# Three token blocks instead of two share each group of first-layer weights, fewer weight tiles are prepared during attention, and attention's output copy moves ahead of the logarithm

## The chip, the cores and the metric

The kernel runs on one core of a Trainium2 chip. The metric is the device time of one execution in microseconds (us). The engines are called PE (matmul), PEld (PE's weight loads), DVE (vector), ACT (scalar activation), POOL (GpSimd) and SP (which here only issues DMAs).

## What is computed

A gated linear attention is followed by two feed-forward layers. The first uses a rational function of the hidden values, the second h times its cosine. The reference, cut to the core:

```python
for t in range(S):                                   # S = 768, B = 4, H = 8, D = 48
    state = alpha[:, :, t, :, None] * state + np.einsum('bhd,bhe->bhde', k[:, :, t], v[:, :, t])
    y[:, :, t] = np.einsum('bhd,bhde->bhe', q[:, :, t], state)
x = y.transpose(0, 2, 1, 3).reshape(B * S, H * D)    # 3072 x 384
h = x @ w_in                                         # 384 -> 2048, weights are float64
P = a[0] + a[1] * h + a[2] * h * h + a[3] * h * h * h
Q = 1.0 + np.abs(b[0]) * np.abs(h) + np.abs(b[1]) * h * h
x = (P / (Q + 1e-06)) @ w_out                        # 2048 -> 384
h = x @ w_in2
out = (h * np.cos(h)) @ w_out2
```

## The kernel before

**Attention** is cut into 24 units (6 chunks of 128 time steps by 4 batches), one unit per slot; slots are numbered n = -3 to 24. A slot's PE work is `scores` (L332), `y_state` (L399), `y_scores` (L409), `update0` (L366) and `transposes` (L354). POOL scales q (L323) and k (L318) and masks two score tiles (L346). DVE and ACT do the decay, its inverse and the copies, and `y_out` (L425) copies a unit's output out of PSUM.

**The first layer** works on 6 blocks of 512 tokens and 16 features (tiles of 128 hidden columns), so it has 96 layer steps n = 0 to 95. Step 0 runs in slot 20: slots 20 to 24 hold attention and layer steps 0 to 4 (LEAD = 20). A step's PE work is `gemm1(n)` (L562: 9 matmuls, three passes for each of 3 parts of the contraction, with x and w split into a high and a low part) and, five steps later, `gemm2` of that tile (L578: 9 matmuls into the three accumulators `acc`). Between the two stands `rational`: on ACT an absolute value, a scaled copy, a logarithm and an exponential (L636, L637, L645, L646) and a rounding (L608); on DVE L628, L631, L632, L633 and L640; on POOL L638, L639 and L613. `gemm1` writes one of four PSUM banks in turn. The bank of tile n - 3 is free once L633 has run in step n, and `gemm1(n + 1)` waits for that.

**The order of blocks.** Blocks 0 and 1 take turns: 11 features of block 0, the same 11 of block 1, then 5 and 5 (`H1 = 11`), so that a feature's weights serve two blocks. A block that is left before its last feature has its sums copied from PSUM to SBUF by ACT (L593), and at its end DVE adds them to the new sums (L597). Blocks 2 to 5 run all 16 features in a row.

**Weights** come as 64-bit floats, a tile at a time (384 KB, one feature of `w_in` or `w_out`). Each is fetched by `w_fetch` (L174) and converted in three "ticks" by `to_f32`: two ACT operations (L72, L73), then DVE L77, then DVE L78. `w_hi` (L215, ACT) rounds it and `w_lo` (L225, POOL) takes the rest. L73 writes a bank that L77 and L78 read. The list `SOME` says how many tiles are fetched in each slot up to 20; from step 5 to step 31 each layer step runs two ticks, so a tile takes a step and a half. Raw tiles land in `spare` (four places) or in `raw` (two).

**The next block's input** is loaded by `x_load`, and split by `x_hi` (L702, ACT) and `x_lo` (L706, DVE), one third in each of three steps: for block 1 in steps 5 to 7, for block 2 in steps 28 to 30.

The order on every engine is the order of the program text; nothing is reordered. DVE, ACT and POOL each run their instructions strictly in a row.

Of the kernel before, what the change touches and what calls it, by code (L numbers as in the profile page):

```python
# [24 lines left out]
NU = NC * B  # L25
H1 = 11
NO = 0
SOME = [0, 0] + 5 * [1, 1, 0] + [1, 1, 1, 2]

# [13 lines left out]
def attn_then_two_moe(ctx, tc, kqT, aT, vP, w1i, w1o, ma, mb, w2i, w2o, out):  # L43
# [70 lines left out]
    kq_t = [kq_all[:, i] for i in range(5)]  # L114
    v_t = [const.tile([128, H * D + 64 - D], F32, tag=f"v{i}", name=f"v{i}") for i in range(4)]
    st_all = const.tile([128, 4, DM], F32, tag="st", name="st")
# [7 lines left out]
    def w_tile(s, f):  # L124
        ws[s][f] = wp.tile([128, 2, DM], F32R, tag=f"w{s}_{f}", name=f"w{s}_{f}")

    w_order = sorted(
        [(0, s, i) for i in range(NF) for s in range(2)],
        key=lambda w: (w[2] + 5 * w[1] + (H1 if w[2] >= H1 else 0), w[1])
    ) + [(1, s, i) for s in range(2) for i in range(NF)]  # L130
    ready = set()
    late = {}
    for i, (_, s, f) in enumerate(w_order[:2 * NF]):
        u = KEEP + i - (2 * NF - (NU - KEEP))
        if u >= KEEP:
# [16 lines left out]

    def in_spare(i):
        return i < sum(SOME[:-1]) and i % 6 < 4

    def w_fetch(upto):

        i = fetched[0]
        fetched[1] = upto
        more = LEAD + 5 <= slot[0] < LEAD + N1  # L160
        most = 4 if more else 2
        if i >= upto or len(steps) > 5 or sum(not in_spare(j) for j in range(i - len(steps), i + 1)) > most:
            return
        w = w_order[i]
        fetched[0] += 1
        if in_spare(i):
            flat = spare[:, 2 * DM * (i % 6):2 * DM * (i % 6 + 1)]
        elif more and i % 4 < 2:
            if not raw_a:
                raw_a.append(const.tile([128, 3 * HP * (C + 1)], I32, tag="a", name="raw_a"))  # L170
            flat = raw_a[0][:, 2 * DM * (i % 2):2 * DM * (i % 2 + 1)]
        else:
            flat = raw_p.tile([128, 2 * DM], I32, tag="raw", name="raw")
# [12 lines left out]
    def tick(k, ahead=0):  # L186

        while k and steps and (len(steps) > ahead or fetched[0] == fetched[1]):
# [8 lines left out]
            if i == 2:  # L197
                steps.pop(0)
                stage[w] = t
                to_hi.append(w)  # L200

    def early(m, s, i):

        return NF * s + i if m == 1 and NF * s + i < NF + NO else None

    def w_hi():
        while to_hi:
            m, s, i = w = to_hi.pop(0)
            at = early(m, s, i)
            if ws[s][i] is None:  # L210
                w_tile(s, i)
            hi = ws[s][i][:, 0]
            if at is not None:
                hi = kq_t[at % 3][:, 1].rearrange("p a b -> p (a b)")[:, :DM].bitcast(F32R)
            nc.scalar.activation(out=hi, in_=stage[w], func=AF.Copy)  # L215
            to_lo.append((w, hi))

    def w_lo(engs):
        engs = list(engs)
        while to_lo:  # L220
# [222 lines left out]
    def convert(n, place):  # L443

        if place == 0:
            turn[:] = [0] * 5 if n < 2 else [1, 1, 1, 0, 0]
            if n >= LEAD + 2:
                turn[:] = [1, 1, 1, 0, 1] if n == LEAD + 2 else [1, 0, 1, 0, 1 if n < NU else 0]
            if n == MORE:
                turn[4] = 1  # L450
            if n == MORE + 1:
                turn[:] = [2, 0, 0, 3, 0]
        assert n != LEAD + 2 or place or not steps[0][1]
        tick(turn[place], 2 if n < LEAD else 1)
        turn[place] = 0
# [68 lines left out]
    def where(n):  # L524
        m, r = divmod(n, N1)
        if n < 2 * H1:
            return 0, *divmod(n, H1)
        if n < 2 * NF:
            blk, f = divmod(n - 2 * H1, NF - H1)
            return 0, blk, H1 + f  # L530
        return m, *divmod(r, NF)

    def in_parts(m, blk):
        return m == 0 and blk < 2

# [17 lines left out]
    def gemm1(n):  # L553
        m, blk, f = where(n)
        assert m or (0, 0, f) in ready
        h = h_bank(n)
        x = xt[m, blk]
        i = 0
        for kk in range(NK):
            ks = slice(kk * 128, (kk + 1) * 128)  # L560
            for w, xx in PASSES:
                nc.tensor.matmul(h, ws[0][f][:, w, ks], x[:, xx, kk, :], start=i == 0, stop=i == 8)  # L562
                i += 1
        T[n] = {"h": h}

    def gemm2(n):
        m, blk, f = where(n)
        d = T.pop(n)
        assert m or (0, 1, f) in ready
        first = f == 0 or in_parts(m, blk) and f == H1  # L570
        last = f == NF - 1 or in_parts(m, blk) and f == H1 - 1
        for k in range(NK):
# [10 lines left out]

    outs = []

    def acc_out(most=NK):

        while outs and most:
# [25 lines left out]

    def rational(n):

# [17 lines left out]
        if one:  # L634
# [39 lines left out]
    def x_load(m, blk, kk):  # L674
        if kk == 0 and (m, blk) not in xt:
            xt[m, blk] = x_p.tile([128, 2, NK, TB], F32R, tag="x", name="x")
        x = xt[m, blk][:, 1, kk, :].bitcast(F32)
        ks = slice(kk * 128, (kk + 1) * 128)
# [21 lines left out]
    def x_hi(m, blk, kk):  # L700
        x = xt[m, blk]
        nc.scalar.activation(out=x[:, 0, kk, :], in_=x[:, 1, kk, :].bitcast(F32), func=AF.Copy)  # L702

    def x_lo(m, blk, kk, eng=None):
        hi, lo = (xt[m, blk][:, i, kk, :] for i in range(2))
        (eng or nc.vector).tensor_tensor(out=lo, in0=lo.bitcast(F32), in1=hi.bitcast(F32), op=ALU.subtract)  # L706
# [151 lines left out]
    def w_first(t, a, e, r):  # L858
# [16 lines left out]
        elif t == 3:  # L875
            v = [const.tile([128, 3 * 128], F32R, tag=f"v{i}", name=f"w_v{i}") for i in range(4)]
            hi, lo = v[:2], v[2:]
# [349 lines left out]

    def layers(n):
        slot[0] = n + LEAD
# [14 lines left out]
        rational(n)  # L1244
        cosine_parts(n)
# [14 lines left out]
        i = n - (N1 - NF)  # L1260
        if n < 2 * NF:
# [25 lines left out]
    with tc.manual_schedule():  # L1287
# [17 lines left out]
        for n in range(-3, NU + 1):  # L1305
# [221 lines left out]
```

## Time and profile before

| | before |
|---|---|
| median of 3 runs | 913.98 us (913.88 to 915.51) |
| the profiled execution, its own time | 913.8 us |
| its span, first to last instruction | 912.1 us |
| PE busy, share of the span | 892.4 us, 98% |
| PE's weight loads | 741.2 us, 81% |
| DVE, ACT, POOL busy | 693.9, 697.1, 702.9 us (76%, 76%, 77%) |
| chain that ended last | PE 72%, DVE 8%, ACT 7%, POOL 6%, DMA 4% |

Busy PE time counts overlapping matmuls once, so 98% says only that a matmul was nearly always under way. How well PE is fed is read from the starts of equal pieces of work: of `scores` in attention, of `gemm1` in the layers.

### The profile page before, as it was taken

What the parts mean: (1) busy time and instruction counts of PE and PEld (TensorE: products, weight loads), DVE (VectorE), ACT (ScalarE), POOL (GpSimd) and SP (SyncE); (2) the same over time, 40 slices, a digit from 0 to 9 for tenths busy, and PEclk for the clock granted to TensorE, in tenths of its full rate; (3) what the DMA queues carried; (4) which work ended last, traced back from release to release, by engine and by line L of the source; (5) the groups of instructions that cost most, each with busy time, mean ns of one, the idle gap of its engine ahead of it and who ended that gap; (6) DMA issues with size and microseconds to landing.
All of it is one profiled execution on the core that took longest, in us unless ns stands there. A gap on an engine that the chain in (4) does not pass through costs nothing.

```text
span 912.1 us, 16494 instructions
## 1 busy us (share of the span) xinstructions
PE 892.4 (98%) x5732; PEld 741.2 (81%) x5732; DVE 693.9 (76%) x1247; ACT 697.1 (76%) x1302; POOL 702.9 (77%) x699
## 2 busy tenths in 40 slices
PE   7999999999999999999999999999999999999997
PEld 7788777887788888888888888878888888888885
DVE  7989799998999989989979767666366554555552
ACT  5999898989889788888788778656577666666653
POOL 6899998999889888889879668669787475655332
PEclk9999999999999999999999999999999999999999
DMA  8999545211233141232165276630243433533432
GB/s 281 357 366 370 191 124 196 82 63 36 104 107 94 57 142 45 87 107 94 53 205 185 95 238 239 202 110 27 74 134 109 161 113 96 167 102 105 139 105 90
DMA packets 67307, 128.87 MB, mean 141 GB/s; under 512 B 6928, under 2 KB 30224, under 8 KB 67216
## 3 DMA queue, kind: packets, MB, share of 16 engines
q1 hardware_dynamic: 67216, 127.74, 43.1%
q8 instruction: 47, 0.77, 0.4%
q14 instruction: 44, 0.36, 0.1%
HBM read 95.21 MB, written 32.51 MB: 140 GB/s over the span
## 4 chain that ended last, share of the span: by engine, by line
PE 72%; DVE 8%; ACT 7%; POOL 6%; DMA 4%; issue 2%; SPq 0%; DVEq 0%; ACTq 0%
PE acc L578 22%; PE b L562 18%; PE acc L1054 15%; PE b L1019 6%; PE r L1019 5%; PE r L562 4%; POOL kq L323 2%; POOL kq L318 2%; DMA kq<-kqT 2%; DVE g L628 1%; DVE z L631 1%; ACT b L645 1%; DVE g L640 1%; DMA a<-aT 1%; PE b L1198 1%
## 5 line engine op out<-in xcount | busy, mean ns | idle before, releaser
L578 PE MATMUL acc<-hi,w 128*128 128x512 f32 x738 | 252.5, 396 | 0.0
L562 PE MATMUL b<-x,w 128*128 128x512 f32 x927 | 233.8, 397 | 1.3 <-DVE g L633 1.1
L613 POOL TENSOR_TENSOR lo<-g,hi 128x512 fp32r<-128x512 f32 x128 | 170.2, 1330 | 66.2 <-ACT hi L608 59.4
L562 PEld LDWEIGHTS b<-x,w 128*128 128x128 f32 x927 | 173.4, 188 | 45.4 <-DVE g L633 4.1
L578 PEld LDWEIGHTS acc<-hi,w 128*128 128x128 f32 x738 | 138.7, 188 | 33.9
L1111 POOL TENSOR_TENSOR lo<-g,hi 128x512 fp32r<-128x512 f32 x64 | 83.0, 1297 | 103.6 <-ACT hi L1110 91.6
L578 PE MATMUL acc<-lo,w 128*128 128x512 f32 x369 | 145.7, 395 | 0.0
L639 POOL TENSOR_TENSOR z<-z,ah 128x512 f32<-128x512 f32 x96 | 124.7, 1299 | 8.0
L1054 PE MATMUL acc<-hi,w_out 128*128 128x512 f32 x384 | 130.3, 395 | 0.0
L608 ACT ACTIVATE hi<-g 128x512 fp32r<-128x512 f32 x128 | 80.4, 628 | 47.8 <-PE acc L578 32.6
L578 PEld LDWEIGHTS acc<-lo,w 128*128 128x128 f32 x369 | 69.4, 188 | 16.5
L638 POOL TENSOR_SCALAR z<-ah,cq 128x512 f32<-128x512 f32 x96 | 74.4, 775 | 5.5 <-ACT ah L636 5.4
L1054 PE MATMUL acc<-lo,w_out 128*128 128x512 f32 x192 | 76.4, 398 | 0.4 <-POOL lo L1111 0.2
L1054 PEld LDWEIGHTS acc<-hi,w_out 128*128 128x128 f32 x384 | 68.7, 188 | 9.9
L640 DVE TENSOR_TENSOR g<-g,b 128x512 f32<-128x512 f32 x72 | 49.1, 682 | 16.2 <-ACT g L637 16.0
L636 ACT ACTIVATE ah<-b 128x512 f32<-128x512 f32 x72 | 42.8, 594 | 19.9 <-PE b L562 19.6
L562 PE MATMUL r<-x,w 128*128 128x512 f32 x225 | 56.8, 397 | 1.0 <-DVE g L633 1.0
L1096 DVE SCALAR_TENSOR_TENSOR ah<-z,b 128x512 f32<-128x512 int32 x44 | 30.2, 685 | 35.9 <-ACT z L1092 35.9
L637 ACT ACTIVATE g<-b,cq 128x512 f32<-128x512 f32 x72 | 56.1, 779 | 0.0
L633 DVE SCALAR_TENSOR_TENSOR g<-g,cq,b 128x512 f32<-128x512 f32 x72 | 53.9, 748 | 2.5
L628 DVE SCALAR_TENSOR_TENSOR g<-g,cq,b 128x512 f32<-128x512 f32 x72 | 53.4, 742 | 0.5
L645 ACT ACTIVATE b<-z,lnb 128x512 f32<-128x512 f32 x72 | 50.1, 696 | 4.7 <-DVE g L628 4.0
(202 smaller groups left out, 2028.7 us busy)
## 6 DMA issues: line engine op xcount, KB each, us to landing
w_out<-wd SPq DMA_DIRECT2D x64, 384.0 KB, 3.1
kq<-kqT SPq DMA_DIRECT2D x24, 512.0 KB, 6.6
w<-wd SPq DMA_DIRECT2D x16, 384.0 KB, 3.1
wd<-w SPq DMA_DIRECT2D x16, 384.0 KB, 2.6
a<-aT SPq DMA_DIRECT2D x23, 258.0 KB, 5.8
raw<-w2o SPq DMA_DIRECT2D x14, 384.0 KB, 3.9
v<-vP SPq DMA_DIRECT2D x24, 192.0 KB, 6.6
x<-x1d SPq DMA_DIRECT2D x18, 256.0 KB, 4.2
```

The source lines that it names most:

```text
L562: nc.tensor.matmul(h, ws[0][f][:, w, ks], x[:, xx, kk, :], start=i == 0, stop=i == 8)
L578: nc.tensor.matmul(acc[k], ws[1][f][:, w, ks], d[g], start=first and i == 0, stop=last and i == 2)
L608: nc.scalar.activation(out=t["hi"], in_=t["g"], func=AF.Copy)
L613: eng.tensor_tensor(out=t["lo"], in0=t["g"], in1=t["hi"].bitcast(F32), op=ALU.subtract)
L628: nc.vector.scalar_tensor_tensor(g, g, cq[:, 3:4], two["h"], ALU.add, ALU.mult)
L638: nc.gpsimd.tensor_scalar(zz, ah, cq[:, 1:2], cq[:, 0:1], ALU.mult, ALU.add)
L639: nc.gpsimd.tensor_tensor(out=zz, in0=zz, in1=ah, op=ALU.mult)
L640: nc.vector.tensor_tensor(out=g, in0=g, in1=h, op=ALU.mult)
L645: nc.scalar.activation(out=r, in_=two["z"], func=AF.Ln, scale=LN_S, bias=lnb)
L1019: nc.tensor.matmul(tile[:, half], w[p], x[q], start=start and i == 0, stop=True, skip_group_check=True)
L1054: nc.tensor.matmul(acc[k], item["w"][:, w, ks], item[g], start=first, stop=last)
L1111: nc.gpsimd.tensor_tensor(out=p["lo"], in0=p["g"], in1=p["hi"].bitcast(F32), op=ALU.subtract)
```

## The change

The three first blocks take turns, over 6, 5 and 5 features (`TURN = 3`, `OFFS`), so blocks 0 to 2 fill steps 0 to 47. Sums that leave PSUM after the first group are copied by ACT (9 copies, in steps 11, 17 and 23), after the second group DVE adds them to what is stored (9 adds, steps 28, 33 and 38), after the third DVE adds and writes the result (9 adds, steps 43, 48 and 53). Before there were 6 copies (steps 16 and 27) and 6 adds (steps 32 and 37), and block 2's result was copied by ACT.

Fetches of slots 2, 3, 5 and 19 and one of two in slot 20 go; raw tiles land in the weight tile's own place. First-layer conversion runs on to step 37, the second layer's starts in step 44 (`S2`). A step that splits x, or that follows an add, runs one tick instead of two. Block 1's x is split in steps 3 to 5 and is wanted by `gemm1(6)`; block 2's in steps 9 to 11 and is wanted by `gemm1(12)`; block 2's x lies in the places of attention's `a` and `v`.

`y_out` of slots 20 to 24 is issued inside `rational`, between the scaled copy and the logarithm.

```diff
-H1 = 11
+H1 = 6
+OFFS = 0, 6, 11, NF
-SOME = [0, 0] + 5 * [1, 1, 0] + [1, 1, 1, 2]
+TURN = 3
+S2 = 44
+SOME = [0] * 6 + 5 * [1, 0, 1]
...
+            flat = wp.tile([128, 2 * DM], I32, tag=f"w{w[1]}_{w[2]}", name="raw")
...
             if f < NF - 1:
-                nc.scalar.activation(out=part(blk, k), in_=acc[k], func=AF.Copy)
+                if group(f) == 0:
+                    nc.scalar.activation(out=part(blk, k), in_=acc[k], func=AF.Copy)
+                else:
+                    added[0] = slot[0]
+                    nc.vector.tensor_tensor(out=part(blk, k), in0=part(blk, k), in1=acc[k], op=ALU.add)
                 continue
...
+        if between:
+            between()
         if two:
             r = two["h"]
             nc.scalar.activation(out=r, in_=two["z"], func=AF.Ln, scale=LN_S, bias=lnb)
...
-        if n < NF:
-            nxt, at, load = (0, 1), n - 5, n == 3
-        elif n < 2 * NF:
-            at, load = n - 2 * NF + 4, n == 2 * NF - 6
+        if n < 2 * NF:
+            nxt, at, load = ((0, 1), n - H1 + 3, n == 0) if n < H1 else ((0, 2), n - 9, n == H1)
...
-        if n < 2 * NF:
+        if n < S2:
             if n > 1:
-                tick(2 if n > 4 else 1, 1)
+                tick(2 if n > 4 and not split and added[0] < slot[0] else 1, 1)
         elif n < N1 - NF:
             if not split:
-                tick(1, 1)
+                tick(2 if added[0] < slot[0] else 1, 1)
...
-                layers(n - LEAD)
-                y_out(n - 1)
+                layers(n - LEAD, partial(y_out, n - 1))
```

On POOL in attention, slots 7 and 8 (`kq<-kq,p` is the scaling of q, `kq<-kq,z` of k, `w<-st` the low part of a weight tile), before:

```order
L323 TENSOR_TENSOR kq<-kq,p 128x512
L318 TENSOR_TENSOR kq<-kq,z 128x512
L225 TENSOR_TENSOR w_0_110<-st,w_0_110 128x384
L346 AFFINE_SELECT hi<-hi 128x512
L346 AFFINE_SELECT lo<-lo 128x512
L323 TENSOR_TENSOR kq<-kq,p 128x512
L318 TENSOR_TENSOR kq<-kq,z 128x512
L225 TENSOR_TENSOR w_1_111<-st,w_1_111 128x384
L346 AFFINE_SELECT hi<-hi 128x512
L346 AFFINE_SELECT lo<-lo 128x512
```

The weight operation is gone from slots 7, 8 and 10 and from one place in slot 21; the first one now stands in slot 11, and from there to slot 20 the pattern is that of before.

On ACT in slot 22, layer step 2 (`ah<-b` is the absolute value, `b<-z,lnb` the logarithm, `yo<-y` the output copy of `y_out`, `hi<-sc` the next slot's first mask copy), now:

```order
L657 ACTIVATE ah<-b_1905 128x512
L658 ACTIVATE g<-b_1905,cq 128x512
L435 ACTIVATE yo<-y 128x512
L668 ACTIVATE b_1830<-z,lnb 128x512
L669 ACTIVATE b_1830<-b_1830 128x512
L225 ACTIVATE w_3_2006<-st 128x384
L75 ACTIVATE st<-raw 128x384
L76 ACTIVATE r_2011<-raw 128x384
```

Before, the copy stood behind the last of these, five instructions later.

On DVE in steps 27 and 28 (`g<-g,cq,b` first is L628 of before, the fourth of a step is L633, `st<-raw` the last tick of a weight tile, `kq<-kq,acc` the new adds), now:

```order
L649 SCALAR_TENSOR_TENSOR g<-g,cq,b_3065 128x512
L652 SCALAR_TENSOR_TENSOR z<-z,b_3024 128x512
L653 SCALAR_TENSOR_TENSOR b_3024<-z,b_3024 128x512
L654 SCALAR_TENSOR_TENSOR g<-g,cq,b_3024 128x512
L661 TENSOR_TENSOR g<-g,b_3109 128x512
L81 SCALAR_TENSOR_TENSOR st<-raw,r_3150 128x384
L613 TENSOR_TENSOR kq<-kq,acc_3005 128x512
L613 TENSOR_TENSOR kq<-kq,acc_3009 128x512
L613 TENSOR_TENSOR kq<-kq,acc_3013 128x512
L649 SCALAR_TENSOR_TENSOR g<-g,cq,b_3109 128x512
L652 SCALAR_TENSOR_TENSOR z<-z,b_3065 128x512
```

The three adds stand ahead of step 28's first operation, so everything of that step on DVE, the operation that frees PE's bank among it, comes after them.

## Rows read from the trace of the kernel before

**Rows 1.** Windows: PE, PEld, DVE, ACT, POOL busy, clock, DMA share, GB/s.

```profile
60.00:80.00 20.00, 18.96 (x391) 16.86 (x389) 17.79 (x49) 18.48 (x38) 19.72 (x23) 1.00 1.06 332
160.00:180.00 20.00, 20.00 (x87) 16.14 (x86) 19.29 (x32) 18.75 (x36) 18.75 (x19) 1.00 0.30 86
```

**Rows 2.** Timeline of PE in attention, `scores` alone: start, length, [idle before <-releaser].

```profile
61.10 1.10 PE L332 MATMUL sc<-kq 48*64 48x128 f32 x32 [0.35 <-POOL kq L318]
65.07 1.10 PE L332 MATMUL sc<-kq 48*64 48x128 f32 x32
69.67 1.10 PE L332 MATMUL sc<-kq 48*64 48x128 f32 x32 [0.34 <-POOL kq L318]
```

**Rows 3.** Timeline of POOL in attention, slots 4 to 12, single operations.

```profile
29.82 1.28 POOL L323 TENSOR_TENSOR kq<-kq,p 128x512 f32<-128x512 f32 x1 [0.58 <-DMA kq<-kqT]
...
35.56 1.27 POOL L323 TENSOR_TENSOR kq<-kq,p 128x512 f32<-128x512 f32 x1 [2.05 <-DMA kq<-kqT]
...
64.97 1.00 POOL L225 TENSOR_TENSOR w<-st,w 128x384 fp32r<-128x384 f32 x1
```

**Rows 4.** DMA queues, 20 to 100 us: packets, MB, share of 16 engines.

```profile
q1 hardware_dynamic: 14997, 28.13, 99.7%
```

**Rows 5.** Timeline of PE and ACT, slots 22 and 23.

```profile
114.27 1.09 PE L399 MATMUL y<-kq,s 48*64 48x128 f32 x16 [1.34 <-ACT yo L425]
...
113.63 0.59 ACT L425 ACTIVATE yo<-y 128x512 f32<-128x512 f32 x1
```

**Rows 6.** Timeline of DVE, layer steps 4 and 5.

```profile
119.92 0.74 DVE L628 SCALAR_TENSOR_TENSOR g<-g,cq,b 128x512 f32<-128x512 f32 x1
...
122.02 0.75 DVE L633 SCALAR_TENSOR_TENSOR g<-g,cq,b 128x512 f32<-128x512 f32 x1
...
127.44 1.14 DVE L706 TENSOR_TENSOR x<-x 128x512 fp32r<-128x512 f32 x1 [0.58 <-ACT x L702]
```

**Rows 7.** Timeline of PE, `gemm1` of steps 6, 11, 27, 28, 29, 33, 34.

```profile
127.14 2.26 PE L562 MATMUL b<-x,w 128*128 128x512 f32 x9
...
150.20 2.27 PE L562 MATMUL r<-x,w 128*128 128x512 f32 x9
...
217.41 2.27 PE L562 MATMUL r<-x,w 128*128 128x512 f32 x9
221.61 2.27 PE L562 MATMUL b<-x,w 128*128 128x512 f32 x9
226.63 2.37 PE L562 MATMUL b<-x,w 128*128 128x512 f32 x9 [0.67 <-DVE g L633]
...
244.60 2.37 PE L562 MATMUL b<-x,w 128*128 128x512 f32 x9 [0.46 <-DVE g L633]
248.90 2.26 PE L562 MATMUL b<-x,w 128*128 128x512 f32 x9
```

**Rows 8.** Timeline of DVE, layer steps 24 to 33.

```profile
205.59 0.74 DVE L628 SCALAR_TENSOR_TENSOR g<-g,cq,b 128x512 f32<-128x512 f32 x1
...
209.81 0.74 DVE L628 SCALAR_TENSOR_TENSOR g<-g,cq,r 128x512 f32<-128x512 f32 x1
...
213.65 0.74 DVE L628 SCALAR_TENSOR_TENSOR g<-g,cq,b 128x512 f32<-128x512 f32 x1
...
218.07 0.74 DVE L628 SCALAR_TENSOR_TENSOR g<-g,cq,b 128x512 f32<-128x512 f32 x1
...
223.25 0.56 DVE L77 SCALAR_TENSOR_TENSOR r<-st,r 128x384 int32<-128x384 int32 x1 [1.73 <-ACT r L73]
223.72 0.74 DVE L628 SCALAR_TENSOR_TENSOR g<-g,cq,b 128x512 f32<-128x512 f32 x1
...
236.53 0.74 DVE L628 SCALAR_TENSOR_TENSOR g<-g,cq,b 128x512 f32<-128x512 f32 x1
...
241.69 0.74 DVE L628 SCALAR_TENSOR_TENSOR g<-g,cq,b 128x512 f32<-128x512 f32 x1
...
245.17 0.75 DVE L628 SCALAR_TENSOR_TENSOR g<-g,cq,r 128x512 f32<-128x512 f32 x1
```

More of the change, by code (lines that the diff above doesn't have):

```diff
@@ L114, in attn_then_two_moe @@
     kq_t = [kq_all[:, i] for i in range(5)]
-    v_t = [const.tile([128, H * D + 64 - D], F32, tag=f"v{i}", name=f"v{i}") for i in range(4)]
+    VW = H * D + 64 - D
+    v_all = const.tile([128, 4, VW], F32, tag="v", name="v")
+    v_t = [v_all[:, i] for i in range(4)]
     st_all = const.tile([128, 4, DM], F32, tag="st", name="st")
@@ L125, in w_tile, with group @@
         ws[s][f] = wp.tile([128, 2, DM], F32R, tag=f"w{s}_{f}", name=f"w{s}_{f}")
+    def group(f):
+        return sum(f >= i for i in OFFS[1:-1])
     w_order = sorted(
         [(0, s, i) for i in range(NF) for s in range(2)],
-        key=lambda w: (w[2] + 5 * w[1] + (H1 if w[2] >= H1 else 0), w[1])
+        key=lambda w: (w[2] + 5 * w[1] + (TURN - 1) * OFFS[group(w[2])], w[1])
     ) + [(1, s, i) for s in range(2) for i in range(NF)]
@@ L159, in w_fetch @@
         fetched[1] = upto
-        more = LEAD + 5 <= slot[0] < LEAD + N1
-        most = 4 if more else 2
-        if i >= upto or len(steps) > 5 or sum(not in_spare(j) for j in range(i - len(steps), i + 1)) > most:
+        if i >= upto or len(steps) > 5:
             return
         w = w_order[i]
-        fetched[0] += 1
[L166 to L173, printed above, removed]
+        if w[0] == 0:
+            if 2 * NF - NU + KEEP <= i > slot[0] - LEAD - 2 + 2 * NF - NU + KEEP:
+                return
+            flat = wp.tile([128, 2 * DM], I32, tag=f"w{w[1]}_{w[2]}", name="raw")
+        else:
+            more = LEAD + TURN * NF + 2 <= slot[0] < LEAD + N1
+            if len(steps) + 1 > (4 if more else 2):
+                return
+            if more and i % 4 < 2:
+                if not raw_a:
+                    raw_a.append(const.tile([128, 3 * HP * (C + 1)], I32, tag="a", name="raw_a"))
+                flat = raw_a[0][:, 2 * DM * (i % 2):2 * DM * (i % 2 + 1)]
+            else:
+                flat = raw_p.tile([128, 2 * DM], I32, tag="raw", name="raw")
+        fetched[0] += 1
         nc.sync.dma_start(out=flat, in_=(w1i, w1o, w2i, w2o)[2 * w[0] + w[1]][w[2]].bitcast(I32))
@@ L200, in tick, with kq_half @@
                 to_hi.append(w)
+    def kq_half(i):
+        return kq_t[i // 2][:, i % 2].rearrange("p a b -> p (a b)")
     def early(m, s, i):
@@ L452, in convert @@
                 turn[:] = [2, 0, 0, 3, 0]
-        assert n != LEAD + 2 or place or not steps[0][1]
+        assert n != LEAD + 2 or place or not (steps and steps[0][1])
         tick(turn[place], 2 if n < LEAD else 1)
@@ L556, in gemm1 @@
         h = h_bank(n)
-        x = xt[m, blk]
+        x = [x_part(m, blk, i) for i in range(2)]
         i = 0
@@ L569, in gemm2 @@
         assert m or (0, 1, f) in ready
-        first = f == 0 or in_parts(m, blk) and f == H1
-        last = f == NF - 1 or in_parts(m, blk) and f == H1 - 1
+        first = f == 0 or in_parts(m, blk) and f in OFFS
+        last = f == NF - 1 or in_parts(m, blk) and f + 1 in OFFS
         for k in range(NK):
@@ L584, in attn_then_two_moe @@
     outs = []
+    added = [0]
     def acc_out(most=NK):
@@ L613, in rest_g, with rational @@
         eng.tensor_tensor(out=t["lo"], in0=t["g"], in1=t["hi"].bitcast(F32), op=ALU.subtract)
-    def rational(n):
+    def rational(n, between=None):
         def tile_at(i):
@@ L674, in x_load @@
     def x_load(m, blk, kk):
-        if kk == 0 and (m, blk) not in xt:
+        if (m, blk) == (0, 2):
+            if kk == 0:
+                for tag, words in (("a", 3 * HP * (C + 1)), ("v", 4 * VW)):
+                    t = const.tile([128, words], F32R, tag=tag, name=f"x_{tag}")
+                    x2.append(t[:, :NK * TB].rearrange("p (a t) -> p a t", a=NK))
+        elif kk == 0 and (m, blk) not in xt:
             xt[m, blk] = x_p.tile([128, 2, NK, TB], F32R, tag="x", name="x")
-        x = xt[m, blk][:, 1, kk, :].bitcast(F32)
+        x = x_part(m, blk, 1)[:, kk].bitcast(F32)
         ks = slice(kk * 128, (kk + 1) * 128)
@@ L875, in w_first @@
         elif t == 3:
-            v = [const.tile([128, 3 * 128], F32R, tag=f"v{i}", name=f"w_v{i}") for i in range(4)]
+            v_w = const.tile([128, 4, VW], F32R, tag="v", name="w_v")
+            v = [v_w[:, i, :3 * 128] for i in range(4)]
             hi, lo = v[:2], v[2:]
@@ L1225, in all_ok1, with layers @@
         nc.vector.tensor_scalar(bad, tot, 128.0 * 2 * NU - 0.5, None, ALU.is_lt)
-    def layers(n):
+    def layers(n, between=None):
         slot[0] = n + LEAD
```

42 lines of the change are left out of this document (20 added, 22 removed).

## Prediction

> **What bounds the kernel now.** I read the windows first [rows 1]. From 160 to 180 us PE is busy for all of 20.00 us, but DVE (19.29), ACT (18.75) and POOL (18.75) are nearly as full; from 60 to 80 us, in attention, POOL is the fullest besides PE. So I looked at the starts of equal work, not at busy time.
>
> In the layers a step without disturbance takes 221.61 - 217.41 = 4.20 us [rows 7]. Where a step is longer, the row names the releaser: `gemm1(29)` and `gemm1(33)` waited for DVE's L633. L633 ends 122.02 + 0.75 - 119.92 = 2.85 us after L628 starts [rows 6]. With L628 at 223.72 [rows 8] that is 226.57, and `gemm1(29)` starts at 226.63 [rows 7]. Hence the rule for this stage: a step lasts 4.20 us, or until 2.91 us after its L628 if that is later. I call the start of L628 after the step's `gemm1` its offset; above 1.29 us PE stalls.
>
> DVE hardly gains on PE while weights are converted: from step 24 to 27 its L628 moves 218.07 - 205.59 = 12.48 us while PE needs 12.60 [rows 8]. In the stage where first-layer weights are converted, work added to DVE, or to an ACT operation that DVE waits for, thus becomes a PE stall after about 0.3 us of slack. Without weight operations a step costs DVE 245.17 - 241.69 = 3.48 us [rows 8], and DVE gains 0.72 a step.
>
> In attention two `scores` starts lie 3.97 us apart where PE runs without a break (61.10 to 65.07) and 4.60 where POOL also has a weight tile (65.07 to 69.67) [rows 2]; L225 takes 1.00 us of POOL [rows 3], which is busy for 19.72 of 20.00 us [rows 1]. Before that, POOL waits for the transfers of k and q: 0.58 and 2.05 us [rows 3], while the DMA queue is busy for 99.7% of 80 us [rows 4].
>
> **Part by part.**
>
> *Fewer tiles in attention.* Three tiles (slots 2, 3, 5) leave the full queue. It moved 28.13 MB in 79.8 busy us, 0.353 MB a us [rows 4]; a tile of 0.393 MB is 1.11 us, three are 3.3 us. On POOL the conversions of slots 7, 8 and 10 go: 3 x (4.60 - 3.97) = 1.9 us, PE's own 3.97 being late next. The DMA waits that vanish sum to 2.6 us. The two gains are the same time seen from two engines where both are full, so they do not add: I take 3.0 us, near the queue's price, with 1.9 (POOL alone) and 2.6 + 1.9 = 4.5 as ends. The two tiles of slots 19 and 20 I cost at nothing: there the next layer steps and attention together keep PE occupied.
>
> The Trainium skill, page "Perfetto Trace Analysis", section "Roofline", says that a single core is bounded by its 16 DMA engines at about 435 GB/s and calls about 120% of 358 GB/s the practical ceiling. By that figure a tile is an estimated 0.90 us, three are 2.7 us, and at 352 GB/s the queue had room, so that POOL's 1.9 us alone would be won. The trace speaks for a full queue: 99.7% busy, and POOL waits for a transfer.
>
> *`y_out` ahead of the logarithm.* PE waited 1.34 us for this copy at 114.27, and it started only at 113.63 [rows 5]. Five ACT operations earlier, the wait goes. But PE gets only as far as the next gate: `gemm1(5)` follows L633 of step 4, which ended at 122.02 + 0.75 = 122.77 [rows 6], a chain through ACT and DVE that the copy didn't hold up. So of 1.34 us I credit nothing by itself. The copy also delays the logarithm, by up to its own 0.59 us.
>
> *The split of x, blocks 1 and 2.* As many operations as before, elsewhere. A split is 1.14 us on DVE at its longest and here also waited 0.58 us for ACT [rows 6]. One now stands in step 3, ahead of L633 of step 4: `gemm1(5)` comes some 0.5 us later. In return steps 5 to 7 lose two thirds of their splits. From `gemm1(6)` to `gemm1(11)` PE took 150.20 - 127.14 = 23.06 us for 21.00 [rows 7], 2.06 lost. I follow L628 by the rule above: it leaves a stall of about 0.45 at step 6 and small ones at step 10 and 11, so that `gemm1(12)` comes 0.7 us earlier against the end of attention than before. Bounds: 0 to 2.0 earlier. Queued behind this wait on DVE are L628 and with it PE; and `gemm1(6)` and `gemm1(12)` now want the last third in the step after its split, where before there was a step or more to spare.
>
> *The old stalls of steps 28 to 33.* 248.90 - 221.61 = 27.29 for six steps of 4.20 [rows 7]: 2.1 us, from copies in step 27, splits, and adds in step 32. That collision goes: -2.1 us.
>
> *Copies by ACT in steps 11, 17, 23.* The nearest row is step 27: three copies, then two ticks on ACT, and L77 waits 1.73 us [rows 8]; L628 moves 223.72 - 218.07 = 5.65 us, where step 24, of the same kind without copies, takes 209.81 - 205.59 = 4.22, so +1.43. Steps 17 and 23 have the same order on ACT and DVE. The offset before them, by the rule after a stall, is about 1.0, so each stalls 1.0 + 5.65 - 4.20 - 1.29 = 1.15. Step 11 has copies and the last third of the split together, behind a full ACT step: 1.6.
>
> *Adds by DVE, 18 for 6.* L628 to L628 with three adds is 241.69 - 236.53 = 5.16, without 3.48 [rows 8]: 1.68 for three. The one tick that is left out gives back at most 0.47 and only in the step after. Steps 28, 33 and 38 lie in the conversion stage: offsets of 1.15, 0.8 and 0.8, a step with one weight operation that waits for nothing of 213.65 - 209.81 = 3.84 [rows 8], so 1.15 + 3.84 + 1.68 - 4.20 - 1.29 = 1.2, then 0.8 and 0.8. Steps 39 to 42 have no weights; DVE gains 0.72 in each and hides the adds of step 43. In steps 48 and 53 the second layer's weights run at two ticks a step: 0.4 and 1.1. ACT's three copies of block 2's result go where ACT isn't late: nothing.
>
> *The sum.* Attention -3.0, steps 3 to 12 -0.7, old stalls -2.1; new: 1.6 + 1.15 + 1.15 + 1.2 + 0.8 + 0.8 + 0.4 + 1.1 = 8.2. Together +2.4 us on the profiled 913.8, 916.2; the median of the runs is 0.2 above the profiled one, so **916.4**. Bounds of the new stalls: nothing, since copies fall in step 16 too and PE runs from 150.20 to 217.41, 16 steps of 4.20, without loss [rows 7]; and the full 3 x 1.43 + 5 x 1.68 = 12.7. I take 8.2 since offsets, not sizes, decide, and a stall resets the offset to about 0.9 each time.
>
> **Rivals.**
>
> *The new work is absorbed* (faster). If DVE leaves steps 3 to 10 with an offset below about -0.5 instead of 1.0, each copy or add of 1.4 to 1.7 us fits under 1.29. Steps 4 to 8 have fewer weight operations, which speaks for it; the 12.48 against 12.60 speaks against, since nothing in between builds a lead. Two stalls may remain: -5.8 + 1.5 = -4.3, 909.7. It decides from the offset in step 10.
>
> *Half of it is absorbed.* Copies as in step 16, adds as now: -5.8 + 5 = -0.8, 913.2.
>
> *x comes late* (slower still). `gemm1(6)` and `gemm1(12)` have no spare step. If ACT is behind by one of its 0.6 us operations more than I assume, PE waits inside `gemm1`, some 1 us each: 918.5.
>
> *DMA is not the bound.* The gain of attention is 1.9, the time 917.5; inside the forecast's own range.
>
> **How the numbers follow.** A measurement of this kernel tells about 0.2% from no change, 912.2 to 915.8. The forecast has 0.45 (own range 914.8 to 918.5: 0.30 above 915.8, 0.15 within), absorbed 0.25, half absorbed 0.15, late x 0.15. So faster 0.25, same 0.15 + 0.15 = 0.30, slower 0.30 + 0.15 = 0.45. The range holds 8 in 10 if it takes in most of the absorbed case and the late x: 909.5 to 920.5.
>
> **What would show it.** In the trace after: `scores` some 3.97 us apart in slots 4 to 10, and no wait of POOL for k and q above 1 us; no wait of PE for `y_out`'s copy; `gemm1` starts 4.20 apart but for single steps of 5 to 6 us right after steps 11, 17, 23, 28, 33, 38 and 53, released by DVE's last operation of the rational. If PE runs from step 12 to 55 without such rows, the absorbed rival holds and my rule for the offset is wrong; if the first `gemm1` comes less than 2 us earlier, the attention term is.

## The result and the profile after

The changed kernel takes 921.52 us, the median of four runs from 920.35 to 922.91, against 914.58 for the kernel before: a ratio of 1.0076, with a 95% interval of 1.0058 to 1.0094. It is 6.9 us slower; the forecast was 2.4 us slower (916.4), and the time lies outside its range, which ended at 920.5. The profiled execution took 920.35 us with a span of 918.6, which is 6.5 more than the span of before.

The starts of `gemm1` in the two traces tell where it went, each compared with the terms of the forecast's sum:

| stretch | after minus before at its end, us | of this stretch | forecast |
|---|---|---|---|
| first `gemm1` (96.15 for 99.08) | -2.93 | -2.93 | -3.0 |
| to `gemm1(13)` (156.50 for 158.61) | -2.11 | +0.82 | +0.9 (-0.7 and 1.6) |
| to `gemm1(28)` (221.95 for 221.61) | +0.34 | +2.45 | +2.3 |
| to `gemm1(34)` (249.24 for 248.90) | +0.34 | 0.00 | -0.1 (-2.1, 1.2 and 0.8) |
| to `gemm1(55)` (339.34 for 337.10) | +2.24 | +1.90 | +2.3 |
| to `gemm1(79)` (441.49 for 437.90) | +3.59 | +1.35 | no term |
| to `gemm1(103)` (544.87 for 538.70) | +6.17 | +2.58 | no term |

Up to step 55 the sum holds, and then two losses come that it has no term for.

PE in attention, `scores` alone, of the changed kernel (start, length, [idle before <-releaser]); it answers to [rows 2]:

```profile
57.05 1.10 PE L342 MATMUL sc<-kq 48*64 48x128 f32 x32
62.10 1.10 PE L342 MATMUL sc<-kq 48*64 48x128 f32 x32 [0.81 <-POOL kq L328]
66.71 1.10 PE L342 MATMUL sc<-kq 48*64 48x128 f32 x32 [0.34 <-POOL kq L328]
```

Slot 12 starts at 57.05 in place of 61.10: from slot 7 to 12 they are 3.97 apart. At slot 13 1.08 us of these 4.05 go again, because POOL waits 1.39 us for that slot's q and k. Some 1.0 us of the lead stands already in slot 1 (13.26 for 14.28), before the old kernel fetches its first weight tile (19.52), and isn't the tiles': the experiment that moves only the output copy has the old tiles, starts slot 4 at 24.67 (changed kernel 24.63, before 25.64), and still has its first `gemm1` at 99.08. POOL and the data's DMA queue over slots 4 to 20, answering to [rows 3] and [rows 4]:

```profile
34.48 1.27 POOL L333 TENSOR_TENSOR kq<-kq,p 128x512 f32<-128x512 f32 x1 [1.85 <-DMA kq<-kqT]
...
59.53 1.28 POOL L333 TENSOR_TENSOR kq<-kq,p 128x512 f32<-128x512 f32 x1 [1.39 <-DMA kq<-kqT]
...
q1 hardware_dynamic: 16212, 27.64, 99.7%
```

POOL still waits 1.85 and 1.39 us for k and q, and the queue is as full as before, with 27.64 MB for 28.13: what the tiles left free, other transfers took.

The same view at the copy of attention's output and at `gemm1(5)`, answering to [rows 5] and [rows 6]. L577 is the old L562, L654 the old L633, L409 the old L399:

```profile
114.12 1.09 PE L409 MATMUL y<-kq,s 48*64 48x128 f32 x16
...
116.17 2.37 PE L577 MATMUL b<-x,w 128*128 128x512 f32 x9
120.68 2.37 PE L577 MATMUL b<-x,w 128*128 128x512 f32 x9 [2.15 <-DVE g L654]
```

The wait for the copy is gone; PE stands 2.15 us at the next gate.

The same view behind steps 17, 23, 27, 32, 37 and 52, answering to [rows 7]:

```profile
177.57 2.26 PE L577 MATMUL b<-x,w 128*128 128x512 f32 x9
182.88 2.37 PE L577 MATMUL r<-x,w 128*128 128x512 f32 x9 [0.95 <-DVE g L654]
187.19 2.27 PE L577 MATMUL b<-x,w 128*128 128x512 f32 x9
...
209.24 2.37 PE L577 MATMUL b<-x,w 128*128 128x512 f32 x9 [0.90 <-DVE g L654]
...
227.33 0.50 PE L577 MATMUL b<-x_a,w 128*128 128x512 f32 x1 [1.02 <-DVE g L654]
...
249.24 2.36 PE L577 MATMUL b<-x,w 128*128 128x512 f32 x9 [0.66 <-DVE g L654]
...
271.16 2.37 PE L577 MATMUL r<-x,w 128*128 128x512 f32 x9 [0.66 <-DVE g L654]
...
335.03 2.37 PE L577 MATMUL b<-x,w 128*128 128x512 f32 x9 [0.63 <-DVE g L654]
```

Each of these stalls was foretold and is released as foretold; only the small one of step 48 (0.4) isn't there. Step 18 lasts 182.88 - 177.57 = 5.31 us; the step after it lasts 4.31, for the same work 0.11 more than 4.20. Some 0.1 us follows each of the seven stalls (step 12's included).

Now what was not foretold. DVE and PE around step 101, where `gemm1` already belongs to the second layer (L761 prepares weights for that layer's fast product, L683 is the cosine's last product, which `gemm1(102)` waits for):

```profile
533.08 0.55 DVE L81 SCALAR_TENSOR_TENSOR st<-raw_a,r 128x384 int32<-128x384 int32 x1
536.61 3.31 DVE L761 TENSOR_TENSOR w_f<-w_f 128x128 f32<-128x128 f32 x4 [2.98 <-DMA w_f<-wf]
539.84 0.68 DVE L683 TENSOR_TENSOR g<-ah,b 128x512 f32<-128x512 f32 x1
...
540.57 2.36 PE L577 MATMUL b<-x,w 128*128 128x512 f32 x9 [2.32 <-DVE g L683]
```

And its transfer on the DMA-issuing engine:

```profile
533.69 1.27 SPq L861 DMA_DIRECT2D w_f<-wf  x3
```

Read from the bottom: PE waits 2.32 us for L683; L683 stands in DVE's queue behind L761; L761 waits 2.98 us for w_f; and w_f is fetched only at 533.69, just after L81 has taken the last raw weight tile out of `raw_a` (533.08 + 0.55). Both names are one place, the tag "a" of the constant pool: whoever wants it next waits for the last reader. In the kernel before, the last conversion out of that place and the preparation stand so:

```profile
524.70 0.55 DVE L78 SCALAR_TENSOR_TENSOR st<-raw_a,r 128x384 int32<-128x384 int32 x1
...
530.45 0.89 DVE L733 TENSOR_TENSOR w_f<-w_f 128x128 f32<-128x128 f32 x4
```

The transfer had been issued at 525.31, and four operations take 0.89 us with no wait. Relative to its own steps the last conversion comes in step 99 there and in step 100 of the changed kernel, one step too late.

### The profile page after: what moved, and what is told of

Read it like the earlier page. It is cut to its first block, busy times and chain, and to the rows that moved or that the text cites. A ratio compares the mean times of both kernels' runs of the same rounds, so it can differ in the third digit from the quotient of the medians.

```text
span 918.6 us, 16517 instructions
## 1 busy us (share of the span) xinstructions
PE 891.6 (97%) x5732; PEld 737.8 (80%) x5732; DVE 704.8 (77%) x1259; ACT 698.8 (76%) x1302; POOL 704.4 (77%) x696
## 4 chain that ended last, share of the span: by engine, by line
PE 53%; DVE 19%; ACT 12%; POOL 7%; issue 4%; DMA 3%; SPq 0%; DVEq 0%; POOLq 0%; ACTq 0%
PE acc L1083 15%; PE acc L593 12%; PE b L577 11%; PE b L1048 6%; PE r L1048 5%; DVE g L649 3%; DVE z L652 3%; DVE g L661 3%; DVE b L653 2%; DMA kq<-kqT 2%; DVE g L654 2%; POOL kq L328 2%; POOL kq L333 2%; ACT b L668 2%; PE r L577 2%
## 5 line engine op out<-in xcount | busy, mean ns | idle before, releaser
L577 PE MATMUL b<-x,w 128*128 128x512 f32 x819 | 207.2, 397 | 7.1 <-DVE g L654 4.7
L577 PEld LDWEIGHTS b<-x,w 128*128 128x128 f32 x819 | 152.7, 188 | 47.6 <-DVE g L654 8.2
L654 DVE SCALAR_TENSOR_TENSOR g<-g,cq,b 128x512 f32<-128x512 f32 x72 | 53.9, 748 | 2.5
L649 DVE SCALAR_TENSOR_TENSOR g<-g,cq,b 128x512 f32<-128x512 f32 x72 | 53.4, 742 | 0.4
L653 DVE SCALAR_TENSOR_TENSOR b<-z,b 128x512 f32<-128x512 f32 x72 | 50.1, 696 | 2.5
L235 POOL TENSOR_TENSOR w<-st,w 128x384 fp32r<-128x384 f32 x48 | 49.8, 1037 | 2.3 <-ACT w L225 1.9
```

What stands on the lines that cost most here:

```text
L577: nc.tensor.matmul(h, ws[0][f][:, w, ks], x[xx][:, kk], start=i == 0, stop=i == 8)
L649: nc.vector.scalar_tensor_tensor(g, g, cq[:, 3:4], two["h"], ALU.add, ALU.mult)
L654: nc.vector.scalar_tensor_tensor(g, g, cq[:, 2:3], r, ALU.add, ALU.mult)
```

## Experiments

The theory after the result: losses add up one by one, each made in a step where extra work meets an engine without a lead; the forecast failed because it priced the second layer's weights up to step 53 only and left out what they do in steps 70 to 78 and the place that they hold (step 101). Rivals stand with each run. The changed kernel gave 921.52 and, repeated (last experiment), 924.92, and the kernel before spread over 4.7 us in 29 runs on one chip: where a median of four to six runs lies within a few us of these, it decides nothing, and the cause is read from the steps of the traces. Below, steps and lines are those of the changed kernel (experiments with two more lines of code count from L600 on two higher).

**Two weight operations a step from 92 to 95.**

```diff
             if i > 3:
-                tick(1, 1)
+                tick(2 if i > 11 else 1, 1)
```

> The changed kernel, with two weight operations a step instead of one from step 92 to 95; nothing else. Theory (a place held too long): step 101 lasts 6.68 us because VectorE stands 2.98 us before the transfer w_f<-wf, which was issued only when the last raw weight tile had left the same place at 533.08; two operations a step clear that place two to three steps earlier. Then the transfer is issued before step 99, the wait of 2.98 us is under 0.3, step 101 lasts 4.20, and the time is 921.5 - 2.4 = 919.1. Rival (the transfer is late or slow because of other transfers in the queue): it is issued earlier but still waited for; step 101 stays above 6 us, the time within 0.5 of 921.5.

Measured: 920.26 us (1.0056 to 1.0094 of before), which by the time alone is no difference from the changed kernel. In the traces the two starts lie 1.07 us apart at the first `gemm1` and 1.08 at `gemm1(101)`; step 101 then lasts 4.20 us in place of 6.68, 2.48 less, and the row of DVE has lost its wait:

```profile
534.04 0.89 DVE L761 TENSOR_TENSOR w_f<-w_f 128x128 f32<-128x128 f32 x4
```

The transfers were issued at 525.96 to 527.19. The place was the cause: the transfer itself is no faster (it landed 2.8 to 3.2 us after its issue, 2.4 to 3.5 in the changed kernel).

**One weight operation a step from step 60.**

```diff
-                tick(2 if added[0] < slot[0] else 1, 1)
+                tick(2 if added[0] < slot[0] and n < 60 else 1, 1)
```

> The changed kernel, with one weight operation a step instead of two from step 60 on. Theory (no lead): steps 70 to 78 lose 1.35 us because VectorE enters them without a lead; with one operation a step it gains about 0.36 us a step, so L649 starts some 2 us or more ahead of its present place at step 69, and steps 70 to 78 last 4.20 each: -1.35, about 920.2, if step 101 stays as it is (6.68); the weight tiles end some steps later, so that step 101 may move either way and has to be read apart. Rival (the copies by ScalarE in step 69 and the splits alone fill ScalarE): the same steps stay above 4.20, gain below 0.4.

Measured: 917.58 us (1.0027 to 1.0056). PE's `gemm1` behind steps 69 to 71 and 76 to 78 of this kernel:

```profile
403.36 2.26 PE L577 MATMUL b<-x,w 128*128 128x512 f32 x9
407.56 2.26 PE L577 MATMUL r<-x,w 128*128 128x512 f32 x9
411.76 2.26 PE L577 MATMUL b<-x,w 128*128 128x512 f32 x9
...
432.75 2.26 PE L577 MATMUL b<-x,w 128*128 128x512 f32 x9
436.95 2.26 PE L577 MATMUL b<-x,w 128*128 128x512 f32 x9
441.15 2.26 PE L577 MATMUL r<-x,w 128*128 128x512 f32 x9
```

All steps last 4.20; 1.35 us come back, as expected. L649 stands 2.57 us ahead of `gemm1(69)` here. It is the lead that counts, more than the work left out in these steps: from step 69 to 71 L649 moves 9.90 us here and 10.07 in the changed kernel. Step 101 went too (2.57 more): with this pace the last conversion out of "a" falls into step 99 again. Two causes, one knob: the pace of second-layer weights.

**No weight operations in the copy steps.** (`copied[0]` notes the step in which ScalarE copies.)

```diff
-                tick(2 if n > 4 and not split and added[0] < slot[0] else 1, 1)
+                tick(0 if copied[0] == slot[0] else 2 if n > 4 and not split and added[0] < slot[0] else 1, 1)
```

> The changed kernel, with no weight operation in steps 11, 17 and 23, in which ScalarE copies a partial result; these operations come later, and conversion ends in step 40 in place of 37. Theory (copy plus weight operations in one step overrun it): steps 18 and 24 fall from 5.31 and 5.26 to at most 4.3, step 12 from 5.31 to 4.6 or 4.8, some 2.7 us in all with the 0.11 us lost after each stall; the postponed operations cost VectorE lead before the adds of step 42, where a new stall of 0.4 us is expected at step 43: -2.3 net, 919.2. Rival (without slack nothing is won by postponing): the gain at 18 and 24 is given back at once in steps 13 to 30, net gain below 0.7.

Measured: 920.57 us (1.0047 to 1.0090), not the 919.2 expected. Steps 18 and 24 gave 1.11 and 1.05, step 28 another 0.86 (its stall is down to 0.3, since the weights have shifted by some operations), and steps 11 and 12 gave 0.45. Between `gemm1(13)` and `gemm1(79)` it is 2.8 us faster than the changed kernel, more than expected: the stall foreseen at step 43 didn't come, L651, the L649 of the changed kernel, stands 0.80 us behind `gemm1(43)`. But behind step 101 something new: step 102 lasts 5.73 us in place of 4.30. Two windows of PE there (busy, granted clock, DMA share, GB/s):

```profile
538.00:540.00 2.00, 1.10 (x3) 0.66 0.90 311
540.00:542.00 2.00, 2.00 (x6) 0.50 0.67 204
```

TensorE's granted clock has fallen to the lower of its two levels (0.50, 1.2 GHz) with the wait of 2.4 us. Step 102 lost 1.43 us by that, so steps 101 and 102 together cost this execution 4.1 us, not 2.6.

**The old number of tiles in attention.**

```diff
-SOME = [0] * 6 + 5 * [1, 0, 1]
+SOME = [0, 0] + 5 * [1, 1, 0] + [1, 1, 1, 2]
```

> The changed kernel, with the old numbers of weight tiles in attention (15 by slot 19, in the old slots) in place of 10. Theory (attention is full, so tiles cost there; in the layers they cost only where no lead is): the first gemm1 starts 2.0 to 4.0 us later, near the 99.1 us of the kernel before; conversion in the layers ends in step 29, so the stalls of steps 33 and 38 (0.82 + 0.11 each) go: net +1.1, 922.6. Rival (the tiles in attention cost nothing, and the earlier start came from something else in the change): the first gemm1 stays within 0.5 of 96.15, and the time falls by the 1.9 us to 919.6.

Measured: 922.98 us (1.0085 to 1.0118). The stalls of steps 33 and 38 went (1.85 us with what follows them), and the first `gemm1` came at 98.20. That is 2.05 after the changed kernel's 96.15, but the first two experiments, which are the same program up to there, had it at 97.22 and 97.23. One trace can't settle this term. Behind step 101 the clock fell here too (1.55 us).

**Only the output copy moved, in the kernel before.**

```diff
-                layers(n - LEAD)
-                y_out(n - 1)
+                layers(n - LEAD, partial(y_out, n - 1))
```

> The kernel before, with only attention's output copy moved ahead of the logarithm (slots 20 to 24). Theory (a second gate): TensorE's wait of 1.34 us for this copy goes, but the time returns as a longer wait of gemm1(5) for L633 of step 4; from the first gemm1 to gemm1(6) it takes 28.1 us as now (127.14 - 99.08), within 0.5, and the time is 914.2, within 0.6. Rival one (the wait was worth its length): 26.7 us, 912.8. Rival two (one long wait instead of two short ones is worse, since TensorE's clock falls after it): a wait above 2 us, a granted clock near 0.5 behind it, 1.5 us more: 915.7.

Measured: 914.22 us (0.9988 to 1.0011): no difference. PE at the copy and at `gemm1(5)`; L399 is the copy's waiter, with no wait now:

```profile
117.06 1.09 PE L399 MATMUL y<-kq,s 48*64 48x128 f32 x16
119.11 2.37 PE L562 MATMUL b<-x,w 128*128 128x512 f32 x9
122.89 2.37 PE L562 MATMUL b<-x,w 128*128 128x512 f32 x9 [1.42 <-DVE g L633]
```

`gemm1(3)` is 1.54 us earlier and `gemm1(5)` 0.04 later than before; from the first `gemm1` to `gemm1(6)` it takes 28.11 us (28.06 before). The 1.34 us have moved, whole, to the next gate.

**The changed kernel without this move.**

```diff
-                layers(n - LEAD, partial(y_out, n - 1))
+                layers(n - LEAD)
+                y_out(n - 1)
```

> The changed kernel, with the output copy put back behind the layer step. Theory: from the first gemm1 to gemm1(6) the changed kernel takes 28.8 us where the clock stays up and 30.4 where it falls in step 5 (two kernels that are the same up to there show each); the wait for the copy returns with some 1.3 us and the wait of gemm1(5) falls from 2.1 to about 1, the sum stays, 28.8, and the clock stays up: the time is 921, at most 1 us below 921.5. Rival (the move gains what the wait was): 30.1 us or more, time 922.8.

Measured: 924.60 us (1.0067 to 1.0129). The waits changed places as expected:

```profile
115.52 1.09 PE L409 MATMUL y<-kq,s 48*64 48x128 f32 x16 [1.28 <-ACT yo L435]
...
124.78 2.37 PE L577 MATMUL b<-x,w 128*128 128x512 f32 x9 [0.52 <-DVE g L654]
```

From the first `gemm1` to `gemm1(6)` it takes 29.10 us, against 28.83 and 28.73 in two traces of the changed kernel: of the wait of 1.28 the move wins 0.4 at most. The time is 3 us above what was expected and no higher than the changed kernel's second series. In the profiled execution, the longest of the four, the first `gemm1` came at 100.38. PE stopped six times from 54 to 97 us, mostly in the middle of a group of matmuls, with nothing to wait for that the profile shows:

```profile
68.27 0.32 PE L376 MATMUL u<-v,g 128*64 128x48 f32 x3 [1.41 <-issue]
75.37 0.87 PE L409 MATMUL b<-kq,s 48*64 48x128 f32 x12 [0.99 <-issue]
```

**Weight operations spread by lead.** (With the line of the copy steps above.)

```diff
-                tick(2 if added[0] < slot[0] else 1, 1)
+                tick(1, 1)
             if i > 3:
-                tick(1, 1)
+                tick(2, 1)
```

> The changed kernel, with the weight operations spread by the lead: none in steps 11, 17 and 23; one a step instead of two from step 44 to 79; two instead of one from step 84 to 95. Theory (each loss is work in a step without a lead; the sum is that of the parts): as with the copies alone, steps 18, 24 and 28 give 2.9; as with one operation a step, steps 70 to 78 give 1.35 and step 101 2.5; and the stall of step 53 (0.8 + 0.1) goes as well: 7.6 less than 921.5, 913.9, no difference from the kernel before. Rival (the same sum of work meets the same limit): stalls appear elsewhere in steps 44 to 100, above 917.

Measured: 917.57 us over ten runs (1.0008 to 1.0047). The parts came as expected: 1.1 at step 18, 1.05 at 24, 0.9 at 28, 0.9 at 53, 1.35 at 70 to 78 and 2.5 at 101. The rival had its share: new stalls in steps 92, 93 and 94, where two operations a step met the split of x and no lead was left:

```profile
498.13 2.36 PE L577 MATMUL b<-x,w 128*128 128x512 f32 x9 [0.48 <-DVE g L656]
502.95 2.37 PE L577 MATMUL b<-x,w 128*128 128x512 f32 x9 [0.36 <-DVE g L656]
509.17 2.36 PE L577 MATMUL r<-x,w 128*128 128x512 f32 x9 [1.76 <-DVE g L656]
```

**Steps 3 and 4 without weight operations.**

```diff
-            if n > 1:
+            if n > 1 and n not in (3, 4):
```

> The changed kernel, without the weight operations of steps 3 and 4 (they come later, up to step 39). Theory: gemm1(5) waits 2.1 us for L654 because VectorE stands two weight operations and a third of the split of x ahead of it; one operation of 0.55 us less ahead of it makes the wait 1.6, and the granted clock then stays at 1.00 in steps 5 and 6, where it fell in two of five traces; gain 0.5 by itself, 2.0 where the clock would have fallen: 920.5. Rival (the chain through ScalarE and GpSimd sets the gate): the wait stays at 2.1.

Measured: 922.56 us (1.0063 to 1.0113), not the 920.5 expected. The gate moved as expected, `gemm1(5)` waits 1.64 us, the clock stayed up, and at step 39 the kernel is 0.65 us ahead of the changed kernel against the first `gemm1`. But the first `gemm1` of the profiled execution came at 99.03: attention had two waits on "issue" of 1.02 and 2.22 us, and the clock fell behind the second.

**Two operations a step only where DVE is ahead.** (Again with the line of the copy steps.)

```diff
-                tick(2 if added[0] < slot[0] else 1, 1)
+                tick(2 if added[0] < slot[0] and 53 < n < 62 else 1, 1)
             if i > 3:
-                tick(1, 1)
+                tick(2 if i < 9 else 1, 1)
```

> As the kernel with the spread weight operations (917.6), but two operations a step only in steps 54 to 61 and 84 to 88, where VectorE is ahead, in place of 84 to 95. Theory: of that kernel's trace steps 92 to 94 lost 0.64 + 0.62 + 2.02 us, because two operations a step and the split of x met there without a lead; these go, the rest stays: 917.6 - 3.3 + 0.3 = 914.6. Rival (conserved work): a loss of over 1.5 us elsewhere in steps 54 to 100; 916 or more.

Measured: 915.16 us over twelve runs (0.9998 to 1.0018): 2.4 us below the one before, steps 92 to 94 last 4.20 each, and the only new stall is 0.41 us in step 61. With the stalls named so far taken out, the changed kernel is the equal of the kernel before.

**The same with 15 tiles in attention.**

```diff
-SOME = [0] * 6 + 5 * [1, 0, 1]
+SOME = [0, 0] + 5 * [1, 1, 0] + [1, 1, 1, 2]
```

> The same with the old 15 weight tiles in attention in place of 10; the two differ in nothing else. Its layers save the stalls of steps 33 and 38, 1.8 us. Theory one (the five tiles cost attention 2 to 3 us, as the profile of the changed kernel says): slower than the one with 10 tiles by 0.2 to 1.2 us. Theory two (the executions of attention scatter by 4 us, and the profile of the changed kernel is at their lower end; over executions the tiles cost 0 to 1 us): faster than the one with 10 tiles by 0.8 to 1.8 us, near 913.

Measured: 915.71 us over twelve runs (1.0003 to 1.0026), 0.55 slower than with 10 tiles (from 0.0 to 1.3, if the twelve runs of each are drawn anew many times): theory one, and theory two, faster by 0.8 or more, is out. Its layers save 1.9 us (steps 28 to 40 of the two traces), so the five tiles cost attention and the steps beside it 0.55 + 1.9 = about 2.5 us, give or take 0.7.

**One tile more and the gate of step 4 together.**

```diff
-SOME = [0] * 6 + 5 * [1, 0, 1]
+SOME = [0] * 6 + 4 * [1, 0, 1] + [1, 1, 1]
...
-            if n > 1:
+            if n > 1 and n not in (3, 4):
```

> As the kernel with 10 tiles and the spread weight operations, with one tile more (slot 19) and no weight operations in steps 3 and 4. Theory: gemm1(5) waits 1.6 us in place of 2.1, the clock stays up there, stalls of steps 10 to 12 change by no more than 0.3 in sum: 0.6 to 1.5 us faster than the first kernel of this group, 913.5. Rival (step 4's gain is lost again in steps 6 to 12, where the postponed operations stand): no difference, within 0.4.

Measured: 914.84 us over twelve runs (0.9988 to 1.0016 of before), 0.3 below the kernel with 10 tiles, no difference by these runs: the rival. `gemm1(5)` waits 1.48 us, but steps 10 and 11 have stalls of 0.4 and 1.1 for it. Its best execution took 911.94, its worst 918.26; no version here beats the kernel before beyond what can be measured.

**The changed kernel again.**

> The changed kernel as it is, once more, to see how its executions scatter. Theory: the first gemm1 comes anywhere between 96 and 100.4, as in the traces of kernels that are the same up to there, and the wait of step 101 is always there; the median is 921.5, within 0.8, with a spread of 2 us or more. Rival (the spread came from the chips): executions of one chip lie within 1 us.

Measured: 924.92 us (1.0096 to 1.0135), four runs from 923.27 to 925.58 on one chip. So the rival, which wants one chip's runs within 1 us, is out; but the median was missed by 3.4 us, and all four lie above all four of the first series. The trace, of the shortest of the four, is 2.9 us longer than that of the first series: 1.96 come from waits on "issue" of 0.56 and 1.44 us in attention (first `gemm1` at 98.11), and 1.54 from the clock at 0.50 behind the wait of step 101, which is there as before; small gains elsewhere take off 0.6. Why the whole second series lies above the first isn't shown.

## Why the prediction was right and wrong

**The rule for the offset was right.** Step 18 shows it: L649 starts 2.41 us behind `gemm1(18)`, 1.12 above the rule's 1.29, and the stall is 1.11. The foretold stalls came in their steps, sized 1.54 (steps 11 and 12; forecast 1.6), 1.11 and 1.06 (1.15 each), 1.18 (1.2), 0.82 and 0.82 (0.8 each) and 0.79 (1.1), the one of step 43 was rightly nothing, and the one of step 48 (0.4) didn't come, as DVE had gained more by then (L649 1.19 us behind `gemm1(48)`). Sum 7.3 for 8.2. The 0.1 us after each stall had no term, about 0.8 in all; that the two errors cancel is luck. The rival of absorbed work is out: in step 10, where it was to be decided, L649 stands 1.27 us behind `gemm1(10)`. So is the rival of a late x: PE waited for it once, 0.17 us inside `gemm1(12)`.

**The output copy was right at nothing**, by a run that moved it alone: 0.9999. What the prediction didn't say is what becomes of its wait: a wait of 1.34 and a short one became one of 2.15.

**Attention was right in the profiled trace (-2.93 for -3.0, a match that owes something to luck), and too high over executions.** Four traces with 10 tiles and no wait on "issue" after the first 40 us start `gemm1` at 96.15, 96.44, 97.22 and 97.23, mean 96.8; four with 15 tiles at 99.08, 99.08, 98.20 and 99.30, mean 98.9: 2.2 us. The one trace with 11 tiles starts at 95.36, before all of these, so single traces scatter by 1 us or more. By the times of the pair that differs in nothing else it is 2.5. Both lie between the bounds of 1.9 and 4.5. But five of nine traces with 10 tiles had such waits and started at 97.9 to 100.4, where on the mean (98.9) nothing of the gain is left, and none of the four with 15 had them. Whether the tiles are the cause of that is open; it is part of what sets the second trace of the changed kernel apart from the first. The sign that the prediction named for this term, no wait of POOL above 1 us for k and q, was wrong: the gain came with waits of 1.85 and 1.39 and a full queue.

The estimate by the Trainium skill ("Perfetto Trace Analysis", section "Roofline") gave POOL's 1.9 us alone; the 2.2 and 2.5 lie between it and the 3.0 that went by the full queue, and don't decide.

**What failed is the end of the sum: it stops at step 55.** The prediction says that the second layer's weights run at two ticks a step and costs this for steps 48 and 53 only. At that pace DVE has no lead when it comes to step 69. ScalarE's three copies and, from step 75, the split of x cost 1.35 us there. The trace of before shows what was given up: it ran at one tick, its L628 started 3.73 us ahead of `gemm1(69)`, and the same copies and splits stalled nothing; the changed kernel's L649 starts 0.07 us behind `gemm1(69)`. Before, and then the changed kernel with the wait in front of `gemm1(78)`:

```profile
392.17 0.74 DVE L628 SCALAR_TENSOR_TENSOR g<-g,cq,r 128x512 f32<-128x512 f32 x1
395.90 2.26 PE L562 MATMUL b<-x,w 128*128 128x512 f32 x9
```

```profile
398.21 0.74 DVE L649 SCALAR_TENSOR_TENSOR g<-g,cq,r 128x512 f32<-128x512 f32 x1
398.14 2.26 PE L577 MATMUL b<-x,w 128*128 128x512 f32 x9
...
437.18 2.37 PE L577 MATMUL b<-x,w 128*128 128x512 f32 x9 [0.36 <-DVE g L654]
```

The prediction priced what the change adds, not the lead that it removes.

**And a moved operation was costed by its own length, not by what it holds.** One tick fewer or more shifts the last conversion out of "a", and behind it wait a transfer, the preparation, the cosine and PE in turn: 2.58 us from a delay of one step. Putting the operations earlier (the first experiment) gave it back.

**What remains is beyond the profiled execution.** The sum of 2.4 with the two missing terms, 1.35 and 2.58, is 6.3 of 6.5 measured in the spans. The median is 1.2 above the profiled time and the second series 3.4 higher still. The profiled 920.35 still lies within the forecast's range; the median is beyond it by these losses. In the second series' trace they are a fall of the clock and waits on "issue", neither in the forecast; the other runs have no trace, and where they lost isn't shown.

## What to carry to other kernels

Follow a moved operation to the end of the place that it holds: list what next uses the same buffer, and who stands in its queue. Price lost lead as well as added work, stage by stage to the last step, since an engine that was ahead hides copies which an engine at its limit doesn't. Before counting a removed wait as won, find the next gate; and where the new wait is longer than the old one, look at the granted clock behind it.

## What the runs showed of the hardware

**Falls of TensorE's clock.** In the traces here PE stood idle 2.0 to 2.4 us at three places: in front of `gemm1(5)`, in front of `gemm1(102)`, and in attention on "issue". Behind 9 of these 16 waits the granted clock fell to 0.50, for 3 to 7 us: 3 of 7, 4 of 6 and 2 of 3; behind the five waits of 1.42 to 1.64 us in front of `gemm1(5)` it never did. A shorter wait isn't always safe, though: in the second trace of the changed kernel the clock fell to 0.50 at 82 us, behind a wait of 1.44 us on "issue". At `gemm1(5)` in the first experiment, the timeline of PE and then its windows (busy, granted clock, DMA share, GB/s); the wait is 2.15 us as in the changed kernel, where the clock stayed at 1.00:

```profile
121.75 3.24 PE L577 MATMUL b<-x,w 128*128 128x512 f32 x9 [2.15 <-DVE g L654]
```

```profile
122.00:124.00 2.00, 2.00 (x8) 0.73 1.01 308
124.00:126.00 2.00, 2.00 (x6) 0.50 1.00 292
```

Step 5 lasts 5.84 us there and 4.31 in the changed kernel: 1.5 us more for the same wait. But by `gemm1(13)` nothing of it is left: from the first `gemm1` to there it takes 60.33 us in that trace and 60.35 in the changed kernel's. While PE was slow, DVE came closer (L649 stands 0.20 us behind `gemm1(6)`, not 1.77), and the stalls of steps 6 to 12 shrank by as much. Behind `gemm1(102)` no stalls follow, and there the 1.4 to 1.6 us stay lost. The kernel before has no wait of PE above 1.34 us after its first 16 us; the change made two such places. That its times spread more for it isn't shown.

**Waits on "issue" lie whole blocks of instructions apart.** In the kernel without the move PE stopped at 54.52, 68.27, 75.37, 82.56, 88.83 and 96.16. Between these the trace holds 512, 256, 256, 256 and 256 instructions of TensorE (matmuls, weight loads and its sequencer's), to within one; in the copies' experiment twice 512, in that of the gate 512, to within one as well. The queue that carries instructions, 20 to 100 us of the changed kernel (packets, MB, share of 16 engines; the data's queue is shown above):

```profile
q8 instruction: 12, 0.20, 0.9%
```

0.20 MB in 12 packets is about 17 kB each. The Trainium skill, page "Runtime: NRT & Kernel Launch", section "Instruction fetch mechanics", says that a sequencer fetches its instructions by DMA in blocks of 16 KiB, 256 instructions, and that crossing into the next is mostly hidden. The counts agree with the block. That the crossing is hidden holds in four of the nine traces with 10 tiles and not in the other five, with waits of up to 2.22 us. That the full queue delays these blocks is argued from the two queues' rows, not shown: no run here took transfers away to see the waits go.
